# Windowed attention before a two-layer MLP: score and value products in tiles of 64 rows by 32 columns instead of 64 by 64

## The chip, the cores and the metric

The kernel runs on one core of a Trainium2 chip. The metric is the device time of one execution in microseconds; a time given alone is the median of three runs. The core's engines are TensorE (PE in the rows, its weight loads PEld), VectorE (DVE), ScalarE (ACT), GpSimdE (POOL) and SyncE (SP), which here only issues DMAs. Matmuls write to PSUM, which has eight banks; the other engines read from there.

## The reference

`q`, `k`, `v` have 4 batches, 8 heads, 768 tokens and 64 values a head, in float32. Each token sees the 96 tokens up to itself and, besides, the first 8 tokens of its sequence, with a bias that grows with the distance.

```
keep  = is_global | is_local            # first 8 tokens; 0 <= rel < 96
dist  = where(is_global & ~is_local, 96, |rel|)
s     = where(keep, q k^T / 8 - slope[head] * dist, -1e9)
a     = exp(s - max) / (sum(exp) + 1e-9)
x     = (a v)                            # [tokens, 512], 3072 tokens
h     = x @ w_in                         # 512 -> 2048
g     = where(h > 0, h, exp(min(h, 0)) - 1)
out   = g @ w_out                        # 2048 -> 512
```

## The kernel before, in words

The 3072 tokens are worked in twelve groups of 256 (two blocks of 128). A group's attention output is made in four head pairs and stored as a high and a low float32r part (`xh`, `xl`). The MLP then runs in 16 slices of 128 hidden columns: `up` (line 705) makes three passes of four 128x256 matmuls into `h`, the other engines apply the activation and split the result into `gh` and `gl`, and `down` (line 725) adds 128x512 matmuls into two output banks `o`. The weights arrive as 64-bit floats and are turned on the chip into float32r high and low parts by ScalarE, VectorE and GpSimdE (`weight`, line 367).

Attention has two paths. The first three groups go through `pair` and `heads32` (lines 405 and 464), which transpose with TensorE. The other nine, 36 units of one head pair and 256 tokens, go through `far` and `turned` (lines 519 and 548), and it is these that the change touches. For such a unit:

- TensorE makes the scores (line 538): for each block of 128 tokens and each half of 64 tokens, 64 rows of head dimension against a window of `LW` = 168 keys (96 back, 64 own, 8 global). The two heads of a pair lie in array rows 0 to 63 and 64 to 127, the two halves of a block in array columns 0 to 63 and 64 to 127, so four tiles of 64x64 share the array. A float32 matmul is two records in the trace.
- VectorE adds the bias table `far0` or `far1` and takes the row maximum (line 564), ScalarE takes the exponential with its sum (line 566), VectorE the reciprocal, GpSimdE clears the 24 columns behind the window and divides (lines 573 and 574), and VectorE turns the result in blocks of 32x32 (line 579) into a tile `tr` of `BLK` = 6 blocks.
- SyncE writes `tr` to a DRAM tile `dd` in two DMAs, one for each half (line 586), and reads it back in four DMAs (line 594) as `pt4`, with keys on the partitions.
- TensorE makes the values (line 610), 16 matmuls of 64x64 tiles, half of them with 128 columns and half with 64; ScalarE and VectorE add the two banks and split the result (`seat`, line 660).

`visit` (line 613) puts the values of unit k-2 and the scores of unit k next to each other on TensorE, in one piece, between the matmuls of the MLP. The tables `far0` and `far1` are built once, in `face` (line 671), before the first visit.

The order on every engine is fixed before the run by `Plan` (line 62): each piece of work has a cost, a due time and the tiles that it reads and writes, and `order` (line 111) picks, engine by engine, the due piece that can start first, and gives out the buffers. A tile's buffer is taken when its first writer is placed. What it decides is an order and semaphores; the chip then runs each engine's list in that order.

Of the kernel before, what the change touches and what calls it, by code (L numbers as in the profile page):

```python
# [16 lines left out]
P = 128  # L17
NG = 8
NL = P - NG
NT = 2  # L20
HW = P // 2
BACKW = 96
LW = HW + BACKW + NG
BLK = 6
# [222 lines left out]
class Kernel:  # L247
# [271 lines left out]
    def far(self, b, gi, hp, xh, xl, due, end, X):  # L519
# [13 lines left out]
        def scores(e):  # L533
            for i in range(NT):
                for r in range(2):
                    for j in range(2):
                        g = slice(j * HW, (j + 1) * HW)
                        nc.tensor.matmul(ss[j].t[r * HW:(r + 1) * HW, i, :LW], q()[g, i * P + r * HW:i * P + (r + 1) * HW],  # L538
                                         k()[g, i * KN + r * HW:i * KN + r * HW + LW], start=True, stop=True)

# [7 lines left out]
    def turned(self, b, hp, t0, ss, due, end, X):  # L548

        nc, p = self.nc, self.plan  # L550
        tr = self.sb("tr", "tr", [P, BLK, 2, NT, 32], slots=X.get("tr"))
# [16 lines left out]
        self.inverse(st, due - 3500, 500.0)  # L568
        for n, pr in enumerate(prs):
# [8 lines left out]
            def turn(e, i=i, j=j, pr=pr):  # L578
                nc.vector.transpose(tr.t[:, :, j, i], pr.t.rearrange("p (b r) -> p b r", r=32))  # L579
# [3 lines left out]
        for half in range(2):  # L583
            def out(e, half=half):
                rows = slice(half * HW, (half + 1) * HW)
                nc.sync.dma_start(dd.t[half:half + 3, rows].rearrange("a p w x -> p a (w x)"), tr.t[rows].rearrange("p (a w) j i r -> p a (w j i r)", w=2))

            outs.append(p.add(sp(), out, [tr], [dd], due - 2000, nbytes=P * 1536, beside=tuple(outs)))
# [10 lines left out]
    def values(self, rest, v, pv):  # L599
# [3 lines left out]
        for i in range(NT):  # L603
            for n in range(2):
                for j in range(2):
                    for g in range(2):
# [3 lines left out]
                        self.nc.tensor.matmul(pv[g].t[j * 64:j * 64 + 64, i].rearrange("p (q r) -> p q r", q=4)[:, q], vv[rows, 2 * i + a, j],  # L610
                                              pt.t[rows, q, a, j, i], start=n == 0, stop=n == 1)

    def visit(self, k, due):
# [6 lines left out]
        if k < N:  # L620
# [4 lines left out]
            cost += 575.0  # L625
# [44 lines left out]

    def face(self, due):
# [5 lines left out]
        def tables(e):  # L677
            t0, t1, g = self.far0.t, self.far1.t, self.g
            on = nc.gpsimd
            for r, at in ((slice(0, HW), BACKW + 32), (slice(HW, P), BACKW - 32)):  # L680
                ii = t1.bitcast(I32)
                on.iota(ii[r, :at + NG], pattern=[[-1, at + NG]], base=BACKW, channel_multiplier=1)
                on.iota(ii[r, at + NG:], pattern=[[-1, LW - at - NG]], base=BACKW - at, channel_multiplier=1)
# [6 lines left out]
            for r, at in ((slice(0, HW), BACKW + 32), (slice(HW, P), BACKW - 32)):  # L690
                on.tensor_copy(t1[r, at:at + NG], g[r])
                nc.vector.memset(t0[r, :at - 32], -BIG)
# [445 lines left out]
```

## Time and profile before

| | before |
|---|---|
| three runs, median (lowest to highest) | 668.13 us (667.91 to 668.93) |
| the profiled execution | 670.26 us, its span 668.5 us |
| TensorE busy in the span | 652.8 us, 98% |
| share of TensorE in the chain that ended last | 87% |
| scores of the later groups (line 538), busy | 27.2 us |
| values of the later groups (line 610), busy | 49.3 us (28.2 + 21.1) |

The span is that of the profiled execution, from its first to its last instruction; the execution's own time is 1.8 us longer, and it lies 2.1 us above the median. Busy time of pipelined matmuls overlaps, so the durations of single records do not add up to the time that they take together. Rows of the timeline give start and duration in microseconds, and a count of merged instructions.

### The profile page before, as it was taken

The numbers are of one execution on the slowest core, as the hardware profiler recorded it, in microseconds if no ns is written. First come the engines' busy times: TensorE is split into PE (matmuls) and PEld (weight loads), VectorE is DVE, ScalarE is ACT, GpSimd is POOL, SyncE is SP. The second block draws the span as 40 slices with busy tenths as digits, with TensorE's granted clock in tenths as the row PEclk, the third lists the DMA queues.
The fourth block names the chain that finished last, engine by engine and source line by source line (L and its number), as shares of the span: only waits on it lengthen the run. The fifth ranks groups of instructions, "written<-read, shape, count | busy, mean of one in ns | idle before, by whom it ended". The sixth has DMA issues, their size and how long they took to land.

```text
span 668.5 us, 15413 instructions
## 1 busy us (share of the span) xinstructions
PE 652.8 (98%) x5584; PEld 565.5 (85%) x5584; DVE 388.4 (58%) x1290; ACT 403.7 (60%) x1209; POOL 152.1 (23%) x411
## 2 busy tenths in 40 slices
PE   9979899999999999999999999999999999999996
PEld 6757688898889889889889889888889888888895
DVE  6988789888575553554564564454464465453232
ACT  6977777665565665665665555565565565554442
POOL 3654665554121111121121121121121111110000
PEclk9999999999999999999999999999999999999999
DMA  8959072400154453344344244255254254030001
GB/s 311 347 183 403 27 285 74 130 1 2 26 166 151 118 143 103 113 117 134 97 127 139 77 131 141 76 142 142 64 157 131 68 165 131 33 96 1 33 1 34
DMA packets 67185, 80.55 MB, mean 121 GB/s; under 512 B 6048, under 2 KB 49312, under 8 KB 67104
## 3 DMA queue, kind: packets, MB, share of 16 engines
q1 hardware_dynamic: 66816, 79.39, 38.0%
q8 instruction: 45, 0.74, 0.5%
q14 instruction: 36, 0.29, 0.1%
q10 hardware_dynamic: 288, 0.13, 0.1%
HBM read 59.05 MB, written 20.45 MB: 119 GB/s over the span
## 4 chain that ended last, share of the span: by engine, by line
PE 87%; DMA 4%; DVE 4%; ACT 2%; issue 2%; POOL 1%; SPq 0%; POOLq 0%; DVEq 0%
PE o L734 40%; PE h L712 38%; PE pv L610 4%; PE s L538 3%; DMA bits<-in_w_in_dram 2%; DMA rk<-in_qkv_dram 1%; DMA rqv<-in_qkv_dram 1%; ACT pr L447 1%; DVE pr L445 1%; DVE g L386 0%; DVE g L382 0%; DVE g L384 0%; DVE st L454 0%; PE s L478 0%; PE pv L484 0%
## 5 line engine op out<-in xcount | busy, mean ns | idle before, releaser
L712 PEld LDWEIGHTS h<-xh,w 128*128 128x128 f32 x1536 | 232.6, 188 | 34.1 <-DVE xh L300 1.3
L734 PE MATMUL o<-w,gh 128*128 128x512 f32 x768 | 245.4, 402 | 0.8 <-ACT gh L298 0.8
L712 PE MATMUL h<-xh,w 128*128 128x256 f32 x1536 | 243.4, 281 | 1.0 <-DVE xh L300 0.9
L720 DVE SCALAR_TENSOR_TENSOR h<-e,h 128x256 f32<-128x256 f32 x192 | 82.1, 428 | 181.4 <-ACT e L719 181.3
L718 ACT ACTIVATE e<-h 128x256 f32<-128x256 f32 x192 | 73.5, 383 | 129.7 <-PE h L712 129.4
L734 PEld LDWEIGHTS o<-w,gh 128*128 128x128 f32 x768 | 129.7, 188 | 25.4 <-ACT gh L298 5.0
L574 POOL TENSOR_SCALAR pr<-pr,st 128x168 f32<-128x168 f32 x144 | 58.8, 408 | 368.3 <-DVE st L455 249.5
L734 PE MATMUL o<-w,gl 128*128 128x512 f32 x384 | 127.7, 395 | 0.0
L712 PE MATMUL h<-xl,w 128*128 128x256 f32 x768 | 121.2, 279 | 0.0
L298 ACT CAST gh<-h 128x256 fp32r<-128x256 f32 x192 | 71.4, 372 | 67.7 <-DVE h L720 66.1
L306 DVE TENSOR_TENSOR gl<-h,gh 128x256 fp32r<-128x256 f32 x192 | 80.1, 417 | 44.3 <-ACT gh L298 43.8
L712 PEld LDWEIGHTS h<-xl,w 128*128 128x128 f32 x768 | 104.1, 188 | 0.0
L719 ACT ACTIVATE e<-e 128x256 f32<-128x256 f32 x192 | 79.9, 416 | 4.6
L566 ACT ACTIVATE pr<-pr,nmax 128x168 f32<-128x168 f32 x144 | 61.5, 428 | 20.6 <-DVE nmax L564 20.6
L734 PEld LDWEIGHTS o<-w,gl 128*128 128x128 f32 x384 | 61.7, 188 | 3.1 <-issue 0.8
L306 POOL TENSOR_TENSOR w<-g,w 128x512 fp32r<-128x512 f32 x32 | 44.0, 1387 | 21.4 <-ACT w L298 21.0
L579 DVE STREAM_TRANSPOSE tr<-pr 128x192 f32<-128x192 f32 x144 | 47.8, 360 | 1.6 <-POOL pr L574 0.3
L564 DVE CUSTOM_DVE_ANT_0 pr<-s,far 128x168 f32<-128x168 f32 x144 | 39.2, 327 | 11.5 <-PE s L538 11.5
L610 PEld LDWEIGHTS pv<-pt,v 64*64 64x64 f32 x1152 | 27.4, 133 | 8.5 <-PE h L712 5.8
L610 PE MATMUL pv<-pt,v 64*64 64x128 f32 (+1 forms) x1152 | 32.3, 250 | 0.0
L306 DVE TENSOR_TENSOR xl<-pv,xh 128x256 fp32r<-128x256 f32 x48 | 20.3, 422 | 17.1 <-ACT xh L298 15.9
L447 ACT ACTIVATE pr<-pr,nmax 128x256 f32<-128x256 f32 (+1 forms) x48 | 23.4, 488 | 7.1 <-DVE nmax L445 7.0
(100 smaller groups left out, 527.9 us busy)
## 6 DMA issues: line engine op xcount, KB each, us to landing
dd<-tr SPq DMA_DIRECT2D x72, 192.0 KB, 2.7
qk<-in_qkv_dram SPq DMA_DIRECT2D x36, 312.0 KB, 3.1
v<-in_qkv_dram SPq DMA_DIRECT2D x36, 256.0 KB, 3.6
pt<-dd SPq DMA_DIRECT2D x72, 128.0 KB, 2.8
bits<-in_w_in_dram SPq DMA_DIRECT2D x16, 512.0 KB, 8.7
bits<-in_w_out_dram SPq DMA_DIRECT2D x16, 512.0 KB, 9.7
out_dram<-ob SPq DMA_DIRECT2D x23, 256.0 KB, 2.0
rqv<-in_qkv_dram SPq DMA_DIRECT2D x12, 384.0 KB, 6.2
```

The costliest lines, as they stand in the source:

```text
L298: self.nc.scalar.copy(out, x)
L306: self.on(e).tensor_tensor(out, x, y, ALU.subtract)
L564: p.add((("DVE", 85 + 1.042 * LW, False),), lambda e, pr=pr, i=i, j=j, h=h, tab=tab, nm=nm: nc.vector.tensor_tensor_reduce(pr.t[:, :LW], s ...
L566: p.add(act(LW, extra=200), lambda e, pr=pr, i=i, j=j, nm=nm: nc.scalar.activation(pr.t[:, :LW], pr.t[:, :LW], AF.Exp, bias=nm, scale=-1.0 ...
L574: nc.gpsimd.tensor_scalar(pr.t[:, :LW], pr.t[:, :LW], st.t[:, n, 2:3], 1.0, ALU.mult, ALU.mult)
L579: nc.vector.transpose(tr.t[:, :, j, i], pr.t.rearrange("p (b r) -> p b r", r=32))
L610: self.nc.tensor.matmul(pv[g].t[j * 64:j * 64 + 64, i].rearrange("p (q r) -> p q r", q=4)[:, q], vv[rows, 2 * i + a, j], pt.t[rows, q, a, ...
L712: nc.tensor.matmul(h.t, w1.t[:, s, cc * P:(cc + 1) * P], x.t[:, cc], start=n == 0 and cc == 0, stop=n == 2 and cc == self.NCC - 1)
L718: p.add(act(W, True), lambda e: nc.scalar.activation(ex.t, h.t, AF.Relu, scale=-1.0), [h], [ex], d - 8000)
L719: p.add(act(W), lambda e: nc.scalar.activation(ex.t, ex.t, AF.Exp, scale=-1.0), [ex], [ex], d - 8000)
L720: p.add(dve(W), lambda e: nc.vector.scalar_tensor_tensor(h.t, ex.t, -1.0, h.t, ALU.add, ALU.max), [h, ex], [h], d - 8000)
L734: nc.tensor.matmul(acc[i].t, g.t[:, i * P:(i + 1) * P], w2.t[:, s], start=fc == f0 and n == 0 and s == HI, stop=fc == f1 - 1 and n == 1)
```

## The change

The tiles of the later groups become 64 rows by 32 columns. `QW` = 32 tokens now share one window, so `LW` falls from 168 to 136 (96 back, 32 own, 8 global) and `BLK` from 6 to 5. The scores are 16 matmuls of 136 columns instead of 8 of 168; each value matmul becomes two, for the two halves of the 64 value columns, 32 matmuls instead of 16. The turned tile keeps 5 written blocks and gets one empty block at each end (`BLK + 2` = 7), which GpSimdE clears with two fills for each unit; an odd quarter of the tokens is written to DRAM from the empty first block on, an even one from the next, so that all quarters land in the same frame of key blocks. The write to DRAM is four DMAs instead of two, with half the packets each. The tables are built for four quarters instead of two halves.

```diff
+QW = P // 4
 BACKW = 96
-LW = HW + BACKW + NG
-BLK = 6
+LW = QW + BACKW + NG
+BLK = 5
...
         def scores(e):
             for i in range(NT):
-                for r in range(2):
+                for r in range(4):
                     for j in range(2):
                         g = slice(j * HW, (j + 1) * HW)
-                        nc.tensor.matmul(ss[j].t[r * HW:(r + 1) * HW, i, :LW], q()[g, i * P + r * HW:i * P + (r + 1) * HW],
-                                         k()[g, i * KN + r * HW:i * KN + r * HW + LW], start=True, stop=True)
+                        nc.tensor.matmul(ss[j].t[r * QW:(r + 1) * QW, i, :LW], q()[g, i * P + r * QW:i * P + (r + 1) * QW],
+                                         k()[g, i * KN + r * QW:i * KN + r * QW + LW], start=True, stop=True)
...
-        tr = self.sb("tr", "tr", [P, BLK, 2, NT, 32], slots=X.get("tr"))
+        tr = self.sb("tr", "tr", [P, BLK + 2, 2, NT, 32], slots=X.get("tr"))
...
+        def ends(e):
+            nc.gpsimd.memset(tr.t[:, 0], 0.0)
+            nc.gpsimd.memset(tr.t[:, BLK + 1], 0.0)
+
+        p.add((("POOL", 250.0, False),), ends, [], [tr], due - 3400)
...
             def turn(e, i=i, j=j, pr=pr):
-                nc.vector.transpose(tr.t[:, :, j, i], pr.t.rearrange("p (b r) -> p b r", r=32))
+                nc.vector.transpose(tr.t[:, 1:BLK + 1, j, i], pr.t.rearrange("p (b r) -> p b r", r=32))
...
-        for half in range(2):
-            def out(e, half=half):
-                rows = slice(half * HW, (half + 1) * HW)
-                nc.sync.dma_start(dd.t[half:half + 3, rows].rearrange("a p w x -> p a (w x)"), tr.t[rows].rearrange("p (a w) j i r -> p a (w j i r)", w=2))
-
-            outs.append(p.add(sp(), out, [tr], [dd], due - 2000, nbytes=P * 1536, beside=tuple(outs)))
+        for r in range(4):
+            def out(e, r=r):
+                rows, half, odd = slice(r * QW, (r + 1) * QW), r // 2, r % 2
+                nc.sync.dma_start(dd.t[half:half + 3, rows].rearrange("a p w x -> p a (w x)"),
+                                  tr.t[rows, 1 - odd:BLK + 2 - odd].rearrange("p (a w) j i r -> p a (w j i r)", w=2))
+
+            outs.append(p.add(sp(), out, [tr], [dd], due - 2000, nbytes=P * 768, beside=tuple(outs)))
...
-                        self.nc.tensor.matmul(pv[g].t[j * 64:j * 64 + 64, i].rearrange("p (q r) -> p q r", q=4)[:, q], vv[rows, 2 * i + a, j],
-                                              pt.t[rows, q, a, j, i], start=n == 0, stop=n == 1)
+                        for d in range(0, 64, QW):
+                            self.nc.tensor.matmul(pv[g].t[j * 64 + d:j * 64 + d + QW, i].rearrange("p (q r) -> p q r", q=4)[:, q],
+                                                  vv[rows, 2 * i + a, j, d:d + QW], pt.t[rows, q, a, j, i], start=n == 0, stop=n == 1)
...
-            cost += 575.0
+            cost += 465.0
...
+    def quarters(self):
+        return [(slice(r * QW, (r + 1) * QW), P - r * QW) for r in range(4)]
...
-            for r, at in ((slice(0, HW), BACKW + 32), (slice(HW, P), BACKW - 32)):
+            for r, at in self.quarters():
                 ii = t1.bitcast(I32)
                 on.iota(ii[r, :at + NG], pattern=[[-1, at + NG]], base=BACKW, channel_multiplier=1)
-                on.iota(ii[r, at + NG:], pattern=[[-1, LW - at - NG]], base=BACKW - at, channel_multiplier=1)
+                if at + NG < LW:
+                    on.iota(ii[r, at + NG:], pattern=[[-1, LW - at - NG]], base=BACKW - at, channel_multiplier=1)
...
-            for r, at in ((slice(0, HW), BACKW + 32), (slice(HW, P), BACKW - 32)):
+            for r, at in self.quarters():
                 on.tensor_copy(t1[r, at:at + NG], g[r])
-                nc.vector.memset(t0[r, :at - 32], -BIG)
+                if at > 32:
+                    nc.vector.memset(t0[r, :at - 32], -BIG)
                 nc.vector.memset(t0[r, at:at + NG], -BIG)
                 nc.vector.tensor_tensor(t0[r, at - 32:at - 32 + NG], t0[r, at - 32:at - 32 + NG], g[r], ALU.max)
```

The costs and the new pieces also move work. On TensorE the list of MLP matmuls between the visits is the same in both kernels except at three visits in a row. The first of these places, before the change: the scores of the fourth unit (`s`), the MLP matmuls behind them, and the start of the values of the third unit (`pv`).

```order
465 L538 MATMUL s_2530<-qk_1598 64x168
466 L734 MATMUL o_2483<-w_528_2400,gh_2498 128x512 x2
467 L712 MATMUL h_2523<-xh_617,w_513_2094 128x256 x4
468 L712 MATMUL h_2523<-xl_624,w_513_2094 128x256 x4
469 L734 MATMUL o_2460<-w_528_2400,gl_2502 128x512
470 L734 MATMUL o_2483<-w_528_2400,gl_2502 128x512
471 L734 MATMUL o_2460<-w_534_2420,gh_2557 128x512 x2
472 L712 MATMUL h_2596<-xh_617,w_519_2168 128x256 x4
473 L734 MATMUL o_2460<-w_534_2420,gl_2559 128x512
474 L712 MATMUL h_2596<-xh_617,w_519_2168 128x256 x4
475 L712 MATMUL h_2596<-xl_624,w_519_2168 128x256 x4
476 L610 MATMUL pv_2620<-pt_379_1924,v_1012 64x128
```

The same place on TensorE with the change:

```order
498 L539 MATMUL s_2598<-qk_1636 32x136
499 L748 MATMUL o_2551<-w_528_2468,gh_2566 128x512 x2
500 L726 MATMUL h_2591<-xh_623,w_513_2186 128x256 x4
501 L726 MATMUL h_2591<-xl_630,w_513_2186 128x256 x4
502 L748 MATMUL o_2528<-w_528_2468,gl_2570 128x512
503 L748 MATMUL o_2551<-w_528_2468,gl_2570 128x512
504 L748 MATMUL o_2528<-w_534_2488,gh_2649 128x512 x2
505 L726 MATMUL h_2690<-xh_623,w_519_2236 128x256 x4
506 L748 MATMUL o_2528<-w_534_2488,gl_2651 128x512
507 L619 MATMUL pv_2700<-pt_379_2008,v_1018 32x128 x2
```

Eight `h` matmuls moved behind the values of the third unit. Between that visit and the values of the fourth unit there are 44 `h` and 19 `o` matmuls instead of 40 and 23, and behind the values of the fourth unit 88 and 46 instead of 84 and 42, so together 4 `h` and 4 `o` matmuls that stood ahead of the fourth unit's values now stand behind them.

The queue of SyncE at the first unit, before the change: the write of `tr` and the four reads behind it.

```order
64 L377 DMA bits_1362<-in_w_out_dram 128x1024
65 L586 DMA dd_1423<-tr_1387 64x3x256 x2
66 L594 DMA pt_316_1516<-dd_1423 64x2x128
67 L594 DMA pt_316_1516<-dd_1423 64x4x128 x2
68 L594 DMA pt_316_1516<-dd_1423 64x2x128
```

And with the change:

```order
64 L378 DMA bits_1388<-in_w_out_dram 128x1024
65 L593 DMA dd_1441<-tr_153 32x3x256 x4
66 L602 DMA pt_316_1536<-dd_1441 64x2x128
67 L602 DMA pt_316_1536<-dd_1441 64x4x128 x2
68 L602 DMA pt_316_1536<-dd_1441 64x2x128
```

Two more writes stand ahead of the reads; the rest of the queue keeps its order in all 36 units. The fills of the empty blocks stand on GpSimdE early in its list: those of the first two units at its very start, and that of the third unit between two subtractions that make low parts of weights:

```order
101 L307 TENSOR_TENSOR w_303_1495<-g_1109,w_303_1495 128x512
102 L572 MEMSET tr_1540 128x128
103 L573 MEMSET tr_1540 128x128
104 L307 TENSOR_TENSOR w_309_1529<-g_1324,w_309_1529 128x512
105 L307 TENSOR_TENSOR w_405_1589<-g_1439,w_405_1589 128x512
```

The third unit's tile has the buffer of the first unit's, so this fill comes after the first unit's four writes have been read out of it.

## Rows read from the trace of the kernel before

**Rows 1.** The page: busy time by engine (us, share of the span, instructions), and the chain that ended last by engine.

```profile
PE 652.8 (98%) x5584; PEld 565.5 (85%) x5584; DVE 388.4 (58%) x1290; ACT 403.7 (60%) x1209; POOL 152.1 (23%) x411
...
PE 87%; DMA 4%; DVE 4%; ACT 2%; issue 2%; POOL 1%; SPq 0%; POOLq 0%; DVEq 0%
```

**Rows 2.** Busy time of each engine in one stretch of the span (from:to, us, then busy (instructions) of PE, PEld, DVE, ACT, POOL, granted clock, DMA share, GB/s).

```profile
92.00:600.00 508.00, 507.89 (x4575) 447.82 (x4574) 289.78 (x958) 303.71 (x914) 102.52 (x319) 1.00 0.38 111
```

**Rows 3.** The groups of TensorE instructions by line and shape, for the products of the later groups (out<-in, tile rows*columns, result partitions x columns, count, busy us, mean ns of one).

```profile
L610 PE MATMUL pv<-pt,v 64*64 64x128 f32 x576 | 28.2, 283 | 0.0
...
L538 PE MATMUL s<-qk 64*64 64x168 f32 x576 | 27.2, 304 | 0.0
...
L610 PE MATMUL pv<-pt,v 64*64 64x64 f32 x576 | 21.1, 217 | 0.0
```

**Rows 4.** TensorE in order of time: the score product of one visit, whose value product began at 398.84 (start, duration of the merged piece, count).

```profile
399.56 0.75 PE L538 MATMUL s<-qk 64*64 64x168 f32 x16
```

**Rows 5.** The same visit through narrow windows of 0.03 to 0.05 us, one answer for each row: every matmul record that runs in the window or earlier in the same unbroken piece is merged, so the count shows how many have started and the duration how far the last of them reaches. The first three rows are the value product, the next three the score product, the last row the last value records.

```profile
398.84 0.34 PE L610 MATMUL pv<-pt,v 64*64 64x128 f32 x4
...
398.84 0.45 PE L610 MATMUL pv<-pt,v 64*64 64x128 f32 x8
...
398.84 0.51 PE L610 MATMUL pv<-pt,v 64*64 64x128 f32 x12
...
399.56 0.33 PE L538 MATMUL s<-qk 64*64 64x168 f32 x4
...
399.56 0.47 PE L538 MATMUL s<-qk 64*64 64x168 f32 x8
...
399.56 0.61 PE L538 MATMUL s<-qk 64*64 64x168 f32 x12
...
399.50 0.24 PE L610 MATMUL pv<-pt,v 64*64 64x64 f32 x4
```

**Rows 6.** The DMA-issuing queue of SyncE: duration of one issue (min/median/max ns) for the write of the turned tile to DRAM and for reading it back, and the time from issue to landing of both.

```profile
L594 SPq DMA_DIRECT2D pt<-dd x144: 586/607/1616, 102.8 to 599.3; - x144
...
L586 SPq DMA_DIRECT2D dd<-tr x72: 589/601/1566, 93.4 to 595.0; - x72
...
DMA to landing us min/median/max: 2.2/2.7/9.4
```

**Rows 7.** The fourth unit of the later groups (the one whose scores begin at 180.02): SyncE issues, and TensorE at its scores and at its values.

```profile
188.23 1.25 SPq L586 DMA_DIRECT2D dd<-tr  x2
...
190.99 3.43 SPq L594 DMA_DIRECT2D pt<-dd  x4
...
180.02 0.75 PE L538 MATMUL s<-qk 64*64 64x168 f32 x16
...
196.66 0.90 PE L610 MATMUL pv<-pt,v 64*64 64x128 f32 x32
```

**Rows 8.** A unit in the steady middle (scores begin at 227.63): SyncE issues, the scores of the next unit, and its own values.

```profile
235.59 1.25 SPq L586 DMA_DIRECT2D dd<-tr  x2
...
238.47 0.33 SPq L526 DMA_DIRECT2D qk<-in_qkv_dram  x1
...
238.90 2.60 SPq L594 DMA_DIRECT2D pt<-dd  x4
...
237.59 0.75 PE L538 MATMUL s<-qk 64*64 64x168 f32 x16
...
244.97 0.90 PE L610 MATMUL pv<-pt,v 64*64 64x128 f32 x32
```

**Rows 9.** The start, where the bias tables of the later groups are built and the first scores follow: VectorE, GpSimdE, SyncE and TensorE in order of time, the idle time before a piece and what ended it in brackets.

```profile
75.79 0.14 DVE L692 MEMSET far<- 64x96 f32 x1 [2.12 <-POOL far L689]
...
76.17 0.17 DVE L694 TENSOR_TENSOR far<-far,tabg 64x8 f32<-64x8 f32 x1
...
86.47 0.42 DVE L300 CAST xh<-pv 128x256 fp32r<-128x256 f32 x1
...
71.24 0.20 POOL L683 IOTA far<- 64x96 int32 x1
...
98.04 1.43 POOL L306 TENSOR_TENSOR w<-g,w 128x512 fp32r<-128x512 f32 x1 [1.28 <-ACT w L298]
...
102.77 2.60 SPq L594 DMA_DIRECT2D pt<-dd  x4
...
78.51 0.93 PE L484 MATMUL pv<-pt,rqv 128*64 128x128 f32 x8 [1.17 <-ACT pt L298]
...
90.52 1.20 PE L734 MATMUL o<-w,gh 128*128 128x512 f32 x4 [0.81 <-ACT gh L298]
```

**Rows 10.** The costliest groups of the page: the other engines' work on one unit (count, busy us, mean ns of one, idle before it).

```profile
L574 POOL TENSOR_SCALAR pr<-pr,st 128x168 f32<-128x168 f32 x144 | 58.8, 408 | 368.3 <-DVE st L455 249.5
...
L579 DVE STREAM_TRANSPOSE tr<-pr 128x192 f32<-128x192 f32 x144 | 47.8, 360 | 1.6 <-POOL pr L574 0.3
...
L564 DVE CUSTOM_DVE_ANT_0 pr<-s,far 128x168 f32<-128x168 f32 x144 | 39.2, 327 | 11.5 <-PE s L538 11.5
```

**Rows 11.** GpSimdE: a fill of 128 columns at the start of the program.

```profile
masks.py:197 POOL MEMSET ident<- 128x128 f32 x1 | 0.2, 204 | 0.0
```

**Rows 12.** The chain that ended last, in order of time, in the dense stretch: eight hidden matmuls of the MLP and four of its output (start, us, what, count).

```profile
92.42 0.94 PE h L712 x8
...
95.93 0.93 PE o L734 x4
```

## The prediction

> **What bounds the kernel now.** I read the page first: TensorE is busy for 98% of the span and makes 87% of the chain that ended last [rows 1]. [...]
>
> Next, how a visit spends its time [rows 3, 4]: the value product begins at 398.84, the score product 0.72 us later at 399.56, and the score product's piece is 0.75 long. The records overlap, so mean durations (304, 283, 217 ns) say little; the narrow windows say more [rows 5]. Records start in fours: four score records reach 0.33 us, eight 0.47, twelve 0.61. A wave of four tiles thus takes 0.14 us for 168 columns; in the values a wave takes 0.11 us for 128 columns and 0.06 for 64. Time goes with the columns of a wave, and the four tiles of a wave run at once: 16 score records are 4 waves, 32 value records are 8 waves.
>
> **The change part by part.**
>
> Scores. 32 records of 136 columns. If eight tiles run at once they are again 4 waves, each 0.14 x 136/168 = 0.113 us. That takes 4 x 0.027 = 0.107 us off a unit, and 36 x 0.107 = 3.84 us in all. The time ahead of the first wave and behind the last, where the array passes between tile shapes, is in both kernels; scores and values still have one shape, so no such passage is added.
>
> Values. 64 records, eight at once: 8 waves with the same columns as before, no gain. The bound is how quickly records can start: four of the last values reach 0.24 us with a mean duration of 0.217 [rows 3, 5], four scores 0.33 with 0.304, so three steps take 23 to 26 ns and one step 7.7 to 8.7 ns, with 10 ns of rounding in each row. Eight steps are 62 to 70 ns against 55 to 60 for a wave of 64 columns. So the four short waves of a visit cost between nothing and 4 x 15 = 60 ns more, 0 to 2.2 us over 36 visits. I take +0.2, near the lower end, since the rounding allows steps of 6 ns.
>
> The write to DRAM. SyncE spends 0.60 us on an issue of `dd<-tr` and 0.61 on one of `pt<-dd`, and a write lands 2.7 us after its issue [rows 6]. The middle reads need all writes, so four writes instead of two put the last landing 2 x 0.63 = 1.27 us later, if an issue of half the packets takes as long. Against that, the chain ahead shrinks: four reductions (327 ns at 168 columns, at most 62 less each, I take 33), four divisions (408, at most 78, I take 70) and the last transpose (360, 60) [rows 10], about 0.5 us in all. In a steady unit the reads are held by something else: they stand behind the load of a later `qk` (238.47), which waits for the next scores (237.59, 0.75 long), so they begin at 238.90 and the last one is issued at 240.9 [rows 8]. With the change: writes from 235.1, the fourth issued at 237.0, landed at 239.7; the reads that need it go out then, the last at 241.05, landed at 243.8. The values begin at 244.97. About 1 us of slack is left, so I cost the steady units at +0.1 us in all, for single units in which one issue is slow (up to 1.6 us [rows 6]).
>
> The fourth unit is different [rows 7]. Before, its four reads end at 194.43 (the last issued 0.61 earlier, landed 2.7 later, at 196.5), and its values begin at 196.66: they are just in time. With the change, 4 `h` and 4 `o` matmuls that stood ahead of these values stand behind them. Eight `h` matmuls take 0.94 us of the chain and four `o` matmuls 0.93 [rows 12], that is 0.117 and 0.235 each; so TensorE arrives 4 x 0.117 + 4 x 0.235 = 1.41 us sooner, plus two score products, 0.21. Its tile comes at the earliest as follows: writes from 187.73, the fourth issued at 189.6, landed at 192.3, three reads behind it at 0.65, the last issued at 193.65, landed at 196.4. TensorE arrives at 196.66 - 1.62 = 195.04. It waits 1.4 us; 0.7 if the smaller writes issue in 0.4, 2.2 if one issue is slow again as in before (3.43 for four reads instead of 2.60). I take +1.4. Queued behind the waiting values are the scores of the sixth unit and all MLP matmuls, so the wait is lost.
>
> The start. The tables: VectorE sits idle for 2.12 us until GpSimdE has built them, TensorE then idles 1.17 us at 78.51 and 0.81 at 90.52 behind this chain [rows 9]. GpSimdE makes three more index fills at 0.20 (+0.6); its six full-width operations, from 71.44 to 75.79, shrink by at most 32/168 (-0.8 to 0, I take -0.5). VectorE has 11 small operations instead of 6 that took 0.55 us (+0.46). At the first scores, four reductions give back 0.13, and the cast of `xh` at 86.47 goes to ScalarE, 0.34 us of VectorE's chain to the next piece. Sum +0.1, between -0.6 and +1.1.
>
> The fills. Two fills of 128 columns, 0.20 us each [rows 11], on GpSimdE, which is busy 102.5 of 508 us [rows 2]: nothing. The third unit's fill waits until the first unit's writes have landed, by 102.77 in before; the subtraction at 98.04 ends at 99.47 [rows 9], so GpSimdE may stand for 3.3 us with weight pieces and divisions queued behind. The weights are worked ahead of use, and I cost this at nothing; if that cover is gone, up to 3.3 us once.
>
> Sum: -3.84 + 0.2 + 0.1 + 1.4 + 0.1 = -2.04 us. The profiled execution took 670.26, so 668.2 on its scale; it lies 2.13 above the median of the runs, on whose scale the forecast is 668.13 - 2.04 = 666.1.
>
> **The rivals.**
>
> First, the fourth unit does not wait, because its chain is ahead by more than I give it, or the start gains: -3.84 + 0.2 + 0.1 = 664.6. For it: ScalarE and VectorE have less to do throughout. Against it: landing and arrival were 0.15 us apart before.
>
> Second, the later write shows elsewhere too: if half-size writes land a microsecond later than 2.7, each fourth unit, with about 1 us of slack by the sum above, begins to wait, 8 x 0.2, and the fourth unit waits 2.4: -3.84 + 0.2 + 0.1 + 2.4 + 1.6 = +0.5, 668.6, no change that shows.
>
> Third, and on the other side: TensorE does not keep eight tiles going. The rows show four at once and nothing of eight. The price is on TensorE's own path. It decides from the point where a visit costs more than 2.04/36 = 0.057 us above my sum, for instance when a start takes 10 ns instead of 7: then the short waves last 0.08, 4 x 0.022 = 0.09 us a visit, +3.2 us, 669.3; when only four run at once, scores are 8 waves instead of 4 (+0.45 us a visit) and values 16 instead of 8 (4 x 0.11 + 4 x 0.06 = +0.68), 1.13 x 36 = 41 us, about 707. For it: all eight must be fed from one instruction stream with twice the instructions. Against it: starts of 7 to 9 ns leave room in every wave but the shortest.
>
> The rows show starts within a wave 7.7 to 8.7 ns apart. [...]
>
> **How the numbers follow.** Forecast 0.50, first rival 0.18, second 0.12, third 0.20. A measurement tells about 0.2%, 1.3 us, from no change: faster is below 666.8, slower above 669.5. The forecast lies 0.7 below the first edge: of its 0.50 I count 0.41 as faster, 0.09 as same; the first rival is faster; the second same, but for 0.02 slower; the third 0.17 slower, 0.03 same. That makes 0.59, 0.22 and 0.19. The range: at the low end 664.0, all terms at their good bounds but the start's; at the high end 671.5, which takes in the third rival up to 0.15 us a visit and leaves the far cases out. The forecast with the first two rivals alone would be 664.2 to 668.8.
>
> **What would show it.** In the new profile, waves of eight records, four to a score product, 0.11 us apart, and a score product of 0.6 us instead of 0.75; value products still 0.9 long; TensorE idle for about a microsecond and a half ahead of the fourth unit's values and nowhere else between 92 and 600; reads of `pt` that begin about a microsecond later in the fourth unit, and within 0.3 us in the steady ones. The prediction is wrong if waves hold fewer than eight, if the values stretch, if TensorE waits at each fourth visit, or if it begins its unbroken stretch more than a microsecond away from 92.

## The result and the profile after

The changed kernel took 677.70 us (median of 4 runs, 677.06 to 678.25) against 668.02 us of the kernel before (667.68 to 668.93, 4 runs): 1.0143 times the time, 95% interval 1.0128 to 1.0158, so 9.7 us slower. Forecast were 666.1 us and a range from 664.0 to 671.5.

The first thing to read is the same stretch as in [rows 2], and two pieces of it (columns as there):

```profile
92.00:600.00 508.00, 505.68 (x6153) 446.92 (x6152) 286.78 (x954) 302.00 (x902) 111.18 (x389) 1.00 0.39 110
92.00:130.00 38.00, 36.57 (x344) 31.69 (x342) 34.51 (x83) 25.18 (x69) 22.33 (x40) 1.00 0.49 165
180.00:200.00 20.00, 19.20 (x363) 16.62 (x369) 11.74 (x46) 12.17 (x40) 3.85 (x19) 1.00 0.49 145
```

TensorE is still busy nearly all the time, but 2.2 us of idle time are new (507.89 - 505.68), 1.43 of them between 92 and 130 us and 0.80 between 180 and 200. Behind 205 us it is never idle, and yet the two kernels drift apart: there the visits themselves must have become longer. TensorE in order of time over the visit that answers to [rows 4, 5] (start, duration of the merged piece, count), with the MLP matmul behind it:

```profile
396.38 0.94 PE L619 MATMUL pv<-pt,v 64*32 64x128 f32 x51
...
397.25 0.73 PE L539 MATMUL s<-qk 64*32 64x136 f32 x29
397.91 0.74 PE L748 MATMUL o<-w,gh 128*128 128x512 f32 x2
```

and the end of the visit of [rows 4] in the kernel before, which began at 398.84:

```profile
400.24 0.50 PE L734 MATMUL o<-w,gh 128*128 128x512 f32 x1
```

Call the time from a visit's first record to the next MLP matmul its length: 1.40 us before, 1.53 after, where 1.30 was forecast. The same length in the two visits that have scores alone and the two that have values alone, before (first four rows) and after:

```profile
84.60 0.80 PE L538 MATMUL s<-qk 64*64 64x168 f32 x16
85.33 1.09 PE L484 MATMUL pv<-pt,rqv 128*64 128x128 f32 x16
...
603.31 0.90 PE L610 MATMUL pv<-pt,v 64*64 64x128 f32 x32
604.14 0.73 PE L734 MATMUL o<-w,gh 128*128 128x512 f32 x2
```

```profile
85.20 0.69 PE L539 MATMUL s<-qk 64*32 64x136 f32 x32
85.82 1.09 PE L485 MATMUL pv<-pt,rqv 128*64 128x128 f32 x16
...
611.28 1.05 PE L619 MATMUL pv<-pt,v 64*32 64x128 f32 x64
612.26 0.74 PE L748 MATMUL o<-w,gh 128*128 128x512 f32 x2
```

Scores alone go from 0.731 to 0.624 us (the trace has nanoseconds), the 0.107 of the forecast to the digit. Values alone go from 0.828 to 0.980, and both together from 1.401 to 1.532. Over all visits: 34 x 0.131 - 2 x 0.107 + 2 x 0.152 = +4.54 us.

How it happens is to be seen in narrow windows over the value product of 396.38, as in [rows 5]. The windows end 0.24, 0.38, 0.42, 0.52 and 0.62 us behind its start; the count says how many records have started by then:

```profile
396.38 0.46 PE L619 MATMUL pv<-pt,v 64*32 64x128 f32 x17
...
396.38 0.62 PE L619 MATMUL pv<-pt,v 64*32 64x128 f32 x33
...
396.38 0.81 PE L619 MATMUL pv<-pt,v 64*32 64x128 f32 x40
...
396.38 0.89 PE L619 MATMUL pv<-pt,v 64*32 64x128 f32 x46
```

33 records have started by 0.38 us, and the window that ends at 0.42 has the same 33. Eight tiles at once do work: the first 32 records are four waves of eight within 0.345 us, as forecast. Then TensorE pauses and goes on more slowly: 13 records in 0.20 us, where the first 32 took 0.345.

The new idle time has three places. The first is the start, TensorE and VectorE (in brackets the idle time before and what ended it), and the granted clock of TensorE behind it (from:to, us, busy, clock, DMA share, GB/s):

```profile
78.42 0.93 PE L485 MATMUL pv<-pt,rqv 128*64 128x128 f32 x8 [2.35 <-ACT pt L299]
...
91.19 1.20 PE L748 MATMUL o<-w,gh 128*128 128x512 f32 x4 [0.73 <-ACT gh L299]
```

```profile
75.09 0.14 DVE L706 MEMSET far<- 32x96 f32 x1 [2.63 <-POOL far L702]
```

```profile
78.00:80.00 2.00, 1.58 (x11) 0.99 0.00 0
80.00:82.00 2.00, 2.00 (x9) 0.50 0.00 0
82.00:84.00 2.00, 2.00 (x9) 0.65 0.00 0
```

TensorE idles 2.35 us ahead of 78.42 instead of 1.17 [rows 9], and in the windows behind that idle time its granted clock is 0.50, then 0.65, some 3.4 us at 0.50 in all. From 78.42 to the matmul of 91.19 it takes 12.77 us, in before from 78.51 to 90.52 12.01, although before has 0.50 us of idle time in it (ahead of 83.10) that the changed kernel hasn't.

The second place is the next visits, GpSimdE and TensorE:

```profile
103.77 0.21 POOL L572 MEMSET tr<- 128x128 f32 x1 [4.09 <-DMA dd<-tr]
```

```profile
112.49 0.74 PE L748 MATMUL o<-w,gh 128*128 128x512 f32 x2 [0.59 <-ACT gh L299]
113.49 0.74 PE L726 MATMUL h<-xh,w 128*128 128x256 f32 x4 [0.26 <-DVE gl L307]
...
124.51 0.73 PE L726 MATMUL h<-xh,w 128*128 128x256 f32 x4 [0.58 <-DVE gl L307]
...
191.31 0.74 PE L726 MATMUL h<-xh,w 128*128 128x256 f32 x4 [0.80 <-DVE gl L307]
...
198.96 1.03 PE L619 MATMUL pv<-pt,v 64*32 64x128 f32 x63
```

GpSimdE stands for the landing of a write before it may clear the third unit's tile, and TensorE idles 1.43 us in the visits behind it. The third place is 191.31: 0.80 us, ahead of an `h` matmul that VectorE's chain to `gl` releases, in the stretch from which MLP work moved away. The traces of the runs below bear out that it goes with the order on TensorE: all six of them with the same 44 `h` and 19 `o` matmuls in this place wait for `gl` there (0.36 to 0.92 us), the three with the fills moved have 48 and 23 and wait 0.48 us for `gh`, and those with the order of before don't wait there. The fourth unit's values at 198.96 have no idle time before them; the page's table of DMAs (count, size, us from issue to landing) has the smaller writes landing in 1.9 us:

```profile
dd<-tr SPq DMA_DIRECT2D x144, 96.0 KB, 1.9
```

The ledger, from one profile to the other: visits +4.54 (+4.65 without the first scores, which lie in the next term), start +0.76 and 1.18 of idle time ahead of it, waits 1.43 and 0.80: 8.82 us. The two profiled executions differ by 678.25 - 670.26 = 7.99, but before's fell idle at 78.51 - 1.17 = 77.34 and after's at 78.42 - 2.35 = 76.07, so before's was 1.27 late already: 9.26 us behind that point. 0.44 us is not assigned.

### The profile page after: what moved, and what is told of

The parts are those of the page before. It is cut to its first block, busy times and chain, and to the rows that moved or that the text cites. A ratio compares the mean times of both kernels' runs of the same rounds, so it can differ in the third digit from the quotient of the medians.

```text
span 676.4 us, 19073 instructions
## 1 busy us (share of the span) xinstructions
PE 658.1 (97%) x7312; PEld 571.9 (85%) x7312; DVE 387.3 (57%) x1296; ACT 405.8 (60%) x1207; POOL 162.7 (24%) x489
## 4 chain that ended last, share of the span: by engine, by line
PE 82%; DMA 7%; DVE 5%; POOL 2%; issue 1%; ACT 1%; SPq 1%; POOLq 0%; DVEq 0%; ACTq 0%
PE o L748 37%; PE h L726 36%; PE pv L619 5%; DMA bits<-in_w_in_dram 4%; PE s L539 3%; DMA bits<-in_w_out_dram 1%; DMA dd<-tr 1%; DVE g L385 1%; DMA rk<-in_qkv_dram 1%; DVE g L383 1%; DVE pr L446 1%; POOL w L307 1%; ACT pr L448 0%; DVE st L455 0%; DMA rqv<-in_qkv_dram 0%
## 5 line engine op out<-in xcount | busy, mean ns | idle before, releaser
L581 POOL TENSOR_SCALAR pr<-pr,st 128x136 f32<-128x136 f32 x144 | 55.2, 383 | 214.2 <-ACT gh L299 155.4
L567 ACT ACTIVATE pr<-pr,nmax 128x136 f32<-128x136 f32 x144 | 58.2, 405 | 17.4 <-DVE nmax L565 16.0
L565 DVE CUSTOM_DVE_ANT_0 pr<-s,far 128x136 f32<-128x136 f32 x144 | 35.6, 295 | 23.3 <-PE s L539 23.3
L572 POOL MEMSET tr<- 128x128 f32 x36 | 7.4, 207 | 155.8 <-DMA dd<-tr 95.6
L586 DVE STREAM_TRANSPOSE tr<-pr 128x160 f32<-128x160 f32 x144 | 43.2, 326 | 1.7 <-POOL pr L581 0.6
L619 PEld LDWEIGHTS pv<-pt,v 64*32 64x32 f32 x2304 | 32.0, 106 | 8.6 <-PE h L726 5.8
L619 PE MATMUL pv<-pt,v 64*32 64x128 f32 (+1 forms) x2304 | 37.8, 248 | 0.0
L539 PE MATMUL s<-qk 64*32 64x136 f32 x1152 | 30.5, 280 | 0.0
```

Source lines behind the costliest of these rows:

```text
L539: nc.tensor.matmul(ss[j].t[r * QW:(r + 1) * QW, i, :LW], q()[g, i * P + r * QW:i * P + (r + 1) * QW], k()[g, i * KN + r * QW:i * KN + r * ...
L567: p.add(act(LW, extra=200), lambda e, pr=pr, i=i, j=j, nm=nm: nc.scalar.activation(pr.t[:, :LW], pr.t[:, :LW], AF.Exp, bias=nm, scale=-1.0 ...
L581: nc.gpsimd.tensor_scalar(pr.t[:, :LW], pr.t[:, :LW], st.t[:, n, 2:3], 1.0, ALU.mult, ALU.mult)
L586: nc.vector.transpose(tr.t[:, 1:BLK + 1, j, i], pr.t.rearrange("p (b r) -> p b r", r=32))
L619: self.nc.tensor.matmul(pv[g].t[j * 64 + d:j * 64 + d + QW, i].rearrange("p (q r) -> p q r", q=4)[:, q], vv[rows, 2 * i + a, j, d:d + QW], ...
```

## The experiments

Four runs first: each half of the tile change alone, and the fills.

**Values whole.** The changed kernel with the loop `for d in range(0, 64, QW)` taken out again, so that values run in 64x64 tiles and scores in 64x32.

```diff
-                        for d in range(0, 64, QW):
-                            self.nc.tensor.matmul(pv[g].t[j * 64 + d:j * 64 + d + QW, i]...
+                        self.nc.tensor.matmul(pv[g].t[j * 64:j * 64 + 64, i]...
```

> The changed kernel with the value product in whole tiles of 64x64 again, as before: 32 value records and 32 score records a visit instead of 64 and 32. In the two profiles a visit with values and scores takes 1.401 us before and 1.532 after; the two visits with scores alone take 0.731 and 0.624, the two with values alone 0.828 and 0.980. Theory 'supply': TensorE's instruction stream brings one record (a weight load and a matmul) each 17 ns, and some 32 records stand ready when a visit begins; what lies beyond them comes late. Then 32 value records run from what stands ready, the 32 score records arrive while the values run (0.66 us for 0.53 us of supply), and a visit takes 0.828 + 0.624 - 0.159 = 1.29 us, or up to 1.35 if the step from 64 to 32 columns costs something: 34 x 0.18 to 0.24 + 2 x 0.15 = 6.5 to 8.5 us less than after, 669.2 to 671.2 us. Rival 'array': products of eight small tiles start at 17 ns whenever they stand behind other small tiles, whatever the supply. Then scores behind values stay at about 0.6 us and more, a visit takes 1.40 to 1.45 us, and the result is 673.5 to 675. Rival 'waits': the loss lies in waits, not in the visits: no change, 677.

Measured: 674.81 us, 1.0104 (1.0089 to 1.0120). A visit:

```profile
402.41 0.90 PE L618 MATMUL pv<-pt,v 64*64 64x128 f32 x32
403.24 0.69 PE L539 MATMUL s<-qk 64*32 64x136 f32 x32
403.86 0.74 PE L747 MATMUL o<-w,gh 128*128 128x512 f32 x2
```

The visit takes 1.453 us, and that is 0.828 + 0.624 = 1.452, the two lengths alone put end to end. The scores behind the values run in full waves of eight, 0.624 us as when alone, which no pace of 17 ns would allow: the theory "array" falls by its mechanism, though its time was nearest. What neither had is the passage between tile shapes: in before, values and scores of one shape overlap by 0.158 us (0.731 + 0.828 - 1.401), with two shapes by nothing. The visits explain the run: 52.29 us in all against 55.28, -2.99, and 677.70 - 2.99 = 674.71.

**Values split.** The kernel before with that loop added, and nothing else.

```diff
-                        self.nc.tensor.matmul(pv[g].t[j * 64:j * 64 + 64, i]...
+                        for d in range(0, 64, 32):
+                            self.nc.tensor.matmul(pv[g].t[j * 64 + d:j * 64 + d + 32, i]...
```

> The kernel before with one part of the change: each value matmul split into two of 32 columns (64 value records a visit, eight tiles), scores as before (16 records of 168 columns, four tiles). 'Supply': 32 records run at once (0.35 us), the other 48 come each 17 ns, so the last starts 1.15 us behind the first and a visit takes 1.15 + 0.14 + 0.16 = 1.45 us against 1.401: 34 x 0.05 + 2 x 0.15 = +2.0 us, 670.0 us. 'Array': values 0.98 and the scores unchanged, 1.55 us a visit, +5.4 us, 673.4. 'Waits': the split costs nothing, 668.0.

Measured: 678.10 us, 1.0151 (1.0135 to 1.0166).

```profile
393.92 1.05 PE L611 MATMUL pv<-pt,v 64*32 64x128 f32 x64
394.90 0.80 PE L538 MATMUL s<-qk 64*64 64x168 f32 x16
395.63 0.73 PE L735 MATMUL o<-w,gh 128*128 128x512 f32 x2
```

A visit takes 1.711 us, again the plain sum, 0.980 + 0.731. All three expectations missed, for the same reason. So the split of the values costs 0.152 us in itself, and the passage between two shapes 0.158 more. The changed kernel has one shape again, but its products overlap by 0.072 us alone (0.624 + 0.980 - 1.532). That closes the sum of a visit: 0.152 for the values, 0.107 less for the scores, and 0.086 of overlap lost make +0.131.

**Fills late.** The changed kernel with the two fills inside the unit's first division.

```diff
-        p.add((("POOL", 250.0, False),), ends, [], [tr], due - 3400)
             def divide(e, n=n, pr=pr):
+                if n == 0:
+                    ends(e)
```

> The changed kernel with the two fills of the turned tile moved from a step of their own to the first division of the unit, so that GpSimdE stands for the write's landing only where it divides. After shows TensorE idle for 0.59, 0.26 and 0.58 us at 112.49, 113.49 and 124.51 behind a GpSimdE that stood 4.09 us for the landing at 103.77. If the fills cause this, these 1.4 us go: 676.3. The planner's order of TensorE's work around the third to fifth unit comes out as before again, so the wait of 0.80 us at 191.31 may go too: 675.5. If the waits come from weights that are late for another reason, 677.7 stays. The visits stay at 1.53 us by every theory.

Measured: 675.19 us, 1.0113 (1.0097 to 1.0128), 2.5 us less than the changed kernel. The stretch of 92 to 130 us is whole again. A wait of 0.63 us has come up later, and 0.48 us are left of the wait near 191:

```profile
92.00:130.00 38.00, 38.00 (x359) 33.95 (x358) 33.27 (x83) 26.22 (x73) 22.78 (x41) 1.00 0.49 155
```

```profile
153.81 0.73 PE L749 MATMUL o<-w,gh 128*128 128x512 f32 x2 [0.63 <-ACT gh L299]
...
189.22 0.96 PE L749 MATMUL o<-w,gh 128*128 128x512 f32 x3 [0.48 <-ACT gh L299]
```

The waits at 112 and 124 us were those of the fills. Its waits behind 92 us come to 1.12 us instead of 2.23, which is 1.1 of the 2.5 us gained; the rest is not assigned. Its visits are unchanged (1.533). In this profile TensorE idled 2.32 us at the start and its clock stayed at 1.00, while it was at 0.50 behind 2.35 us in the changed kernel, behind 2.34 us with values whole and behind 2.35 us in the run with both edits below. What decides it stays open.

**Both.** Values whole and fills late in one kernel.

> Both: values in whole tiles and the fills with the first division. 'Supply': 669.2 to 671.2 less 1.4 to 2.2, 667.0 to 669.8; if the start also loses its 0.7 us, 666.3 at best. 'Array': 671.5 to 673.5.

Measured: 672.88 us, 1.0073 (1.0059 to 1.0086): the two gains add up but for 0.6 us (-2.9 and -2.5 make 672.3).

Next, the pace of small records, and the start.

**Short extra matmuls.** Behind each score product 16 matmuls of 8 columns into columns of the score bank that nobody reads, once behind the kernel before (`w` = 64, four tiles), once behind the changed one (`w` = 32, eight tiles).

```diff
+                        nc.tensor.matmul(ss[j].t[r * w:(r + 1) * w, m % 2, 200:208], q()[g, r * w:(r + 1) * w],
+                                         k()[g, 8 * m:8 * m + 8], start=True, stop=True)
```

> The kernel before with 16 extra matmuls behind each score product (32 records of 8 columns, tiles of 64x64, into columns of the score bank that nobody reads). Theory 'supply': a visit of 48 records takes 1.40 us, long enough to bring 80 records at 17 ns behind the 32 that stand ready; so the extra records stand ready when the array is free and start 6.7 ns apart: 32 x 6.7 = 0.21 us a visit, 36 x 0.21 = +7.7 us, 675.7. Theory 'array' (small tiles behind small tiles start 17 ns apart): 0.53 us a visit, +19 us, 687.

Measured: 682.54 us, 1.0217.

```profile
396.38 0.90 PE L616 MATMUL pv<-pt,v 64*64 64x128 f32 x32
397.10 0.75 PE L538 MATMUL s<-qk 64*64 64x168 f32 x16
397.68 0.60 PE L544 MATMUL s<-qk 64*64 64x8 f32 x32
398.20 0.74 PE L740 MATMUL o<-w,gh 128*128 128x512 f32 x2
```

The visit takes 1.818 us, +0.417: a wave of four tiles with 8 columns takes 0.058 us, no less than the 0.056 of a wave with 64 columns.

> The changed kernel with the same 16 extra matmuls of 8 columns (32 records, tiles of 64x32). 'Supply': its visits of 96 records already wait for records, so each added one costs 15 to 17 ns whatever its columns: 0.49 to 0.53 us a visit, +18 to +19 us, 696. If the array alone set the pace, the same 32 records would cost what they cost behind the kernel before, 0.21 us, +7.7, 685.

Measured: 687.63 us, 1.0293; a visit 1.772 us, +0.240. Neither theory has both runs right. The added records cost less behind the changed kernel than behind the kernel before, so a fixed 17 ns a record can't be what holds the changed visits.

**Edges late.** VectorE's part of the bias tables (the last loop of `tables`) in a step of its own, due 3000 ns later, in the changed kernel and in the kernel before.

```diff
-        self.faced = [p.add((("POOL", 4000.0, True),), tables, due=due - 6000.0, ...)]
+        built = p.add((("POOL", 4000.0, True),), tables, due=due - 6000.0, ...)
+        self.faced = [built, p.add((("DVE", 600.0, False),), edges, due=due - 3000.0, after=[built])]
```

> The changed kernel with VectorE's 11 small operations of the bias tables in a step of their own, shortly ahead of the first reductions that read the tables, instead of at once behind GpSimdE's build. In after VectorE stands 2.63 us for the build at 75.09 with the reductions of an earlier group queued behind, TensorE idles 2.35 us ahead of 78.42 and its granted clock is 0.50 from 80 to 82. If VectorE's queue causes this, the idle time and the drop go: -2.35 and about -1.2 us, with some of it lost in later waits: 674.5 to 676. Rival: the start is bound by loads and weights, and the time returns as another wait ahead of 92 us: 677 to 678.

Measured: 672.65 us, 1.0076 (1.0058 to 1.0093), 5.1 us less than the changed kernel and better than expected. TensorE's waits between 60 and 205 us are now

```profile
82.61 0.85 PE L731 MATMUL h<-xh,w 128*128 128x256 f32 x5 [0.47 <-ACT xh L299]
86.70 1.20 PE L753 MATMUL o<-w,gh 128*128 128x512 f32 x4 [1.35 <-ACT gh L299]
93.12 1.20 PE L753 MATMUL o<-w,gh 128*128 128x512 f32 x4 [0.57 <-ACT gh L299]
...
185.28 0.74 PE L731 MATMUL h<-xh,w 128*128 128x256 f32 x4 [0.80 <-DVE gl L307]
```

The 2.35 us are gone, with them the waits at 112 and 124 us, and the granted clock is 1.00 between 60 and 205 us. What is left over the kernel before is 4.5 us. That the visits cost as much (55.28 - 50.74 = 4.54) is a chance agreement, as the next run shows.

> The kernel before with the same move of its 6 small operations. Before idles 1.17 us ahead of 78.51, without a drop of the clock. If VectorE's queue causes it: 668.0 - 1.2 = 666.8; by the rival 668.0.

Measured: 666.54 us, 0.9975 (0.9962 to 0.9988): 1.6 us less than the kernel before. VectorE's queue held the start of the kernel before too. With the same move in both, then, the change costs 6.1 us (672.65 - 666.54): the visits and 1.6 us besides.

**Scores three times.** `for i in [*range(NT)] * 3` in `scores`: every score product is written three times over the same columns.

> The changed kernel with every score product written three times over the same columns (96 score records a visit instead of 32). The two runs with short extra matmuls fitted neither theory: 32 records of 8 columns cost 0.42 us a visit behind the kernel before, and 0.24 behind the changed one. The new theory 'window': only some 32 records can be between entering TensorE's queue and completing, in order; the 33rd enters when the first completes, 0.29 us behind its start, and once the queue has run dry two records (one f32 matmul) enter each 17 ns. A long stream of 136-column records then has its eight tiles busy again after the first stumble: 8 more waves at 0.113 to 0.120 us, 0.90 to 0.96 us a visit, 36 x 0.93 = +33 us, 711. Theory 'supply' (one record each 17 ns for ever): 64 x 0.0167 = 1.07 us a visit, +38.5, 716.

Measured: 718.83 us, 1.0763. The usual visit and one that stood still:

```profile
395.75 0.98 PE L619 MATMUL pv<-pt,v 64*32 64x128 f32 x58
...
398.20 0.73 PE L748 MATMUL o<-w,gh 128*128 128x512 f32 x2
...
408.47 0.46 PE L539 MATMUL s<-qk 64*32 64x136 f32 x15 [0.27 <-issue]
```

The usual visit takes 2.459 us, 0.927 more, eight waves at 0.116: "window" on this point. The total is nearer to "supply" only because some visits take up to 3.98 us, 8.5 us in all above the usual length, with TensorE waiting for nothing that the profile shows ("issue"). No run shows what it waits for there.

> The kernel before with every score product written three times (48 score records of 168 columns instead of 16, tiles of 64x64). By every theory 8 more waves at 0.143 us, 1.14 us a visit, 36 x 1.14 = +41 us, 709.

Measured: 708.15 us, 1.0603; a visit 2.541 us, +1.140, eight waves at 0.1425 as expected. In a long stream of records, then, eight tiles take 0.116 us a wave against 0.1425, the gain that the forecast counted on.

**Four writes.** The kernel before with its two writes to DRAM cut into four.

```diff
-        for half in range(2):
-                rows = slice(half * HW, (half + 1) * HW)
+        for r in range(4):
+                rows, half = slice(r * 32, (r + 1) * 32), r // 2
```

> The kernel before with its two writes to DRAM of a unit cut into four, as the change does, and nothing else. My forecast's term: nothing to +0.2 us, since the reads stand behind the load of a later unit; 668.1. Rival: each fourth unit waits for its tile, 8 x 0.2 and 2.4 us at the fourth: +4 us, 672.

Measured: 668.01 us, the median of eleven runs (a twelfth took 1610.90 us and is left out), against 667.71 us of the kernel before beside it, 1.0009 (1.0000 to 1.0018): between nothing and 1.2 us. There is no wait at each fourth unit; behind 92 us its trace has a single one of more than 0.1 us, 0.46 us ahead of the values at 448.20, which ends with a read of `pt`.

**All three.** The changed kernel with values whole, fills late and edges late.

> The changed kernel with all three edits: values in whole tiles, fills with the first division, VectorE's part of the tables shortly ahead of its use. With the last alone the kernel took 672.65 us, and TensorE no longer waited at 112 and 124 us. If only the visits are left to gain, they give 55.3 - 52.3 = 3.0 us: 669.6. If the fills still cost 0.5 to 1 us: 668.8. It would beat the kernel before (668) only if a visit with 64-column values and 32-column scores were shorter than 1.401 us, and it took 1.453.

Measured: 669.48 us, 1.0026 (1.0016 to 1.0036), near the time expected, with visits that cost 52.29 - 50.74 = 1.55 us more than those of the kernel before (667.71 beside it). Not every wait is gone: TensorE idles 1.52 us ahead of 88.96, and 0.28 and 0.48 us behind 92. So with scores alone in tiles of 32 columns, and with all three edits, the kernel still loses 1.8 us, and more against the kernel before with its edges late (666.54).

Last, two runs on what slows the visit.

**Long first, scores first.** The order inside the visit alone: the value loops exchanged (`for n` outside `for i`, with one accumulation group a bank), or the score product ahead of the value product.

> The changed kernel with the value matmuls of both token groups over 128 columns first, then those over 64 columns (before: 128 and 64 of the first group, then of the second); the same 64 records, tiles of 64x32. The tripled scores showed waves of eight at 0.116 us for as long as they ran, so records can come every 14.5 ns and 'supply' at 17 falls. 'Window': the array stumbles where the first 32 records are used up before the first pair of passes has completed (0.40 us) and the next matmul has entered (0.43 us). With 32 long records in front the array has work until 0.44 us instead of 0.35, so the stumble of 0.08 us goes: a visit 1.45 us instead of 1.53, 36 x 0.08 = 2.9 us less, 674.8. Rival 'short records': records of 64 columns in eight tiles are slow wherever they stand behind the first 32 (eight in 0.13 us instead of 0.055), so that putting all of them there costs more: 16 of them are moved there, 2 x 0.075 us: up to +0.15 us a visit, 677.7 to 683.

Measured: 676.12 us, 1.0125 (1.0104 to 1.0145); a visit 1.484 us in the mean.

> The changed kernel with the score product ahead of the value product in each visit. 'Window': the 32 records in front are the scores, 136 columns, 0.44 us of work, so the stumble goes as above, but all the 64-column records stand behind: 1.45 to 1.50 us a visit instead of 1.53, 674.8 to 676.6. 'Short records': all 32 short records behind the first 32: up to 1.53 + 0.15, 677.7 to 683.

Measured: 677.95 us, 1.0141 (1.0121 to 1.0161); a visit 1.482 us. Both visits got shorter by 0.05 us, where "short records" wanted them longer; the size is 0.05, where 0.08 was expected of the first and 0.03 to 0.08 of the second. For the first the total follows (34 x 0.048 = 1.6 us). For the second the visits give 1.7 us and the total gives none of it back: its waits at 115 to 127 and 194 us come to 2.77 us instead of 2.23, which is 0.5 of it, and the rest is not assigned.

**What the single records say.** An f32 matmul is two records, 32 records are 16 matmuls. Behind the first 17 matmuls the next one starts its weight load at 0.433 us in the value product of the changed kernel, and the second record of the first matmul ends at 0.402 (start 0.133, 0.269 long). With the short matmuls behind scores alone it is 0.447 against 0.417. With the long values first the 26th matmul comes at 0.651, the second record of the 9th ends at 0.620. Each time the two are 17 matmuls apart and the weight load comes 0.030 to 0.031 us behind, and from there one matmul comes each 17 ns. An estimate from these three streams: a matmul enters when the one 17 places ahead is through, so that about 32 records are under way. It is a fit to the modelled ends of records, and no run shows such a limit by itself.

## Why the prediction was wrong

It failed on its third rival's side, which it gave 0.20: TensorE does not keep eight tiles going in these visits. The sum takes a microsecond of TensorE's time in the stretch of [rows 2] for a microsecond at the end; for the visits a run bears that out: with values whole they are 2.99 us shorter in all, and the time 2.89 (677.70 - 674.81).

- **Scores, -3.84 us.** Right in size where scores stand alone (-0.107), and for a partly wrong reason. The last of eight records in a wave starts 0.047 us behind the first, the last of four 0.020: the last wave gains nothing, 0.047 - 0.020 = 0.027 being what its columns save, and the gain that is missing there came from the first wave (0.140 us instead of 0.193 when alone). In the 34 visits with values only 0.02 us of it is left, since the two products there overlap by 0.072 us instead of 0.158, an overlap that the sum had taken as unchanged.
- **Values, +0.2 us.** The step that failed. It bounded the price of 64 records by how quickly records can start (steps of 6 to 8 ns, 0 to 2.2 us), and they do start so, but only the first 32. Measured: +0.152 us a visit alone, more than twice the upper bound of 0.060; and together with the lost overlap a visit is 1.532 instead of 1.300, 0.23 us above the sum. Over all visits that is +4.54 us where -3.64 was forecast (-3.84 + 0.2), 8.2 us of the miss of 11.6. The rows of before could not show it: there a visit has 48 records in four tiles, and its score waves, behind the 32nd record, still come 0.14 us apart [rows 5]. The third rival had named what the fit points to ("one instruction stream with twice the instructions"); the sentence against it looked at the spacing of starts and not at how many of them keep it.
- **The fourth unit, +1.4 us.** The wait is not at its values (198.96). The smaller writes landed sooner (1.9 us against 2.7 [rows 6]), TensorE came later by what it had lost, and the moved work cost 0.80 us at 191.31 instead. That work moved away from a place that it covered holds, by the runs with other orders; place and size do not.
- **The start, +0.1 us.** GpSimdE's build grew by 0.57 us (69.45 to 75.07, before 70.72 to 75.77) and VectorE's small operations by 0.61, 1.18 together, just above the upper bound of 1.1: up to the first full-width operation the build took 0.84 us more where 0.6 was taken for the three index fills, and the narrower operations saved 0.27 instead of 0.5. On top came +0.76 up to 91.19, with the granted clock at 0.50 for 3.4 us, which no term had.
- **The fills, nothing.** The stand of GpSimdE was seen (3.3 us as the worst case, 4.09 measured) and the cover by weights worked ahead was trusted; 1.43 us of it reached TensorE, and moving the fills took 2.5 us off.
- **The writes, +0.1 us.** Right: four writes in the kernel before cost 0 to 1.2 us by their interval.

No one spacing holds for these records: within a wave of eight they start 6 to 7 ns apart (0.047 us from the first to the last), and with scores written three times the 64 added ones come in waves of eight at 0.116 us, 14.5 ns a record.

## What to carry to other kernels

Ask of a packed matmul not only how closely its records start but for how many of them that pace holds: halving the tiles doubles the records, and here it ended with the 32nd record of a visit. Count the passage between tile shapes as a piece of work (0.158 us of overlap lost here). When VectorE stands behind a slow GpSimdE step, look at what is queued behind it: moving six small operations a little later gained 1.6 us on the kernel before (666.54 against 668.17). And compare two kernels with the same repair in both: a repair given to one alone can hide a loss behind a gain that the other could have had as well.

## What the runs showed of the hardware

Beside the estimate of about 32 records under way, which is fitted to three streams:

- Two products of 64x64 tiles overlap by 0.158 us in a visit of the kernel before, two of 64x32 by 0.072 in the changed kernel. With one product in each shape the visit takes the sum of the two lengths (1.453 us with values whole, 1.711 with values split).
- A wave of four 64x64 tiles takes 0.058 us with 8 columns and 0.056 with 64.
- With every score product written three times in the changed kernel, TensorE stood ahead of score records eight times, 5.9 us in all and up to 1.1 at a time, which the profile puts to "issue".
- Behind 2.34 to 2.35 us of idle time at the start, TensorE's granted clock was 0.50 in three profiles (the changed kernel, values whole, and both edits in one); behind 2.32 us in the run with the fills late it stayed at 1.00.
